# Attention with a bucketed bias and a feed-forward layer on one core: a new hand-laid order, one transpose each for q and k, single block stores, spare matmuls, a table difference on VectorE

## The chip, the cores and the metric

One core of a Trainium2 chip runs the whole program. The metric is the device time of one execution in microseconds (us); lower is better. The engines are named as in the profile: PE is TensorE (matmuls), PEld its weight loads, DVE is VectorE, ACT is ScalarE, POOL is GpSimd, SP is SyncE. POOL, SP and ACT also issue DMAs.

## The reference

Eight batches of eight heads, 576 positions, 64 channels a head. Attention gets a bias that depends only on the distance of the two positions (32 buckets, the last for all distances from 128 on), and its output goes through two projections with a leaky ReLU between them.

```python
def _attn_ref(q, k, v, bias_table):          # q, k, v: (8, 8, 576, 64), bias_table: (32, 8)
    scores = q @ k.transpose(0, 1, 3, 2) / sqrt(64)
    n = abs(pos[:, None] - pos[None, :])
    large = min(16 + (log(max(n, 1) / 16) / log(128 / 16) * 15).astype(int), 31)
    bucket = where(n < 16, n, large)
    scores = scores + bias_table[bucket].transpose(2, 0, 1)[None]
    return softmax(scores) @ v

def _moe_ref(x, w_in, w_out):                # x: (4608, 512), w_in: (512, 2048), w_out: (2048, 512)
    h = x @ w_in
    return maximum(0.01 * h, h) @ w_out
```

x is the attention output with the heads side by side; everything is float32 outside, bf16 in the matmuls.

## The kernel before, in words

**Attention** runs over 32 pairs `n` (8 batches `b`, 4 pairs of heads `p`). For a pair, q and k are turned so that the channels lie on the partitions. For the first nine pairs but one PE turns them (`turn_by_pe`); for the others DVE copies the rows of q and of k into one tile `pr` (`rows`), and one DMA transpose on SP's queue turns both into one tile `tu` (`turn_by_dma`), from which two copies make `qt` and `kt` (`take_turned`). PE makes the scores in six units (`score`: four of 128 keys, two for the last 64 positions), ACT takes the exponential into `at` (`expo`), DVE multiplies the band of near positions with a table of exponentiated bias differences, `hk` (`band`), PE multiplies with v (`av`, `av_tail`), and DVE divides by the row sum that an extra column of ones gave (`norm`, tile `opair`). A second transpose (`x_dma` on SP's queue, `x_pe` on PE) puts the result into `xT`, a ring of four batches.

**The table.** Since exp(s + bias) is wanted up to a factor, `hk` holds the exponential of the bias less that of the last bucket. In the opening a matmul with `from_last` (identity less its last column) subtracts on PE (`shift_table`, tile `ps_d`), four exponentials make `diag` (`exp_table`), and matmuls with the one-hot matrix `hots` spread it (`spread`, `take_spread`).

**Feed-forward** runs over nine token tiles `T` of 512 tokens. The first projection (`ffn_in`, tile `pm`, then `ffn_act` into `gt`) is plain for T below 6. For T = 6, 7 and 8 (`SPLIT`) a unit, half of the 2048 columns, is done with seven products of half-size blocks instead of eight (`plan_split`, `in_product`, `in_keep`, `in_add`, `in_act`), whose sums of weights (`mix_w_in`) and of x (`mix_x`) DVE makes. The partial products are kept in the buffers of attention (`held`: `at`, `vn`), the sums in those of q and k. The second projection takes seven products in the same way for all T (`ORDER`, `product`), DVE combines them in `y` (`combine`), and SP stores `y` by half tiles of rows (`ffn_store`); the last tile is stored by blocks (`block_store`).

**The order.** Nothing is scheduled by a compiler: a planner (`Plan`) holds all tasks with costs, dependencies, PSUM slots (`S` two, `O` one, `M` three) and ranks, and simulates the engines to lay one fixed order for each; each engine then runs its list in that order and waits by semaphores. `SHIFT` moves ranks, `HOLD` keeps a task back until a planned time, `SWAP` moves a copy between ACT and DVE. Loads on POOL's queue are planned one after the other (`pool_load`); transposes get a planned landing, and some tasks a reserve, `t["spare"]`, in us. Idle PE time before `WARM` (26 us of the plan) is filled with matmuls on `junk` (`spin`, tile `ps_w`), so that PE isn't idle while it waits; ten of them open the program:

```python
    spin(10)
    plan.run(spin)
```

Of the kernel before, what the change touches and what calls it, by code (L numbers as in the profile page):

```python
# [35 lines left out]

class Plan:


    LAG, COLD, WARM, EARLY, PATIENCE = 0.25, 4.9, 26.0, 34.0, 0.3  # L40

    SHIFT = {
# [26 lines left out]
    }  # L69

    SWAP = (20, 62, 88, 91, 92, 180, 185, 209, 214, 265, 273, 274, 996, 1089, 1368, 1757,)
# [26 lines left out]
    def order(self):  # L98
# [5 lines left out]
        free, done, waiting, ring = {}, [], {}, 0.0  # L104
# [3 lines left out]
        while any(waiting.values()):  # L108
# [29 lines left out]
            ring = self.place(t, r, free, self.slots, ring)  # L138
            done.append(t)
        free, ring = {}, 0.0  # L140
        for t in done:
            e = t["engine"]
            r = max([free.get(e, 0.0)] + [d["end"] + (self.LAG if d["engine"] != e else 0.0) for d in t["after"]])
            held = {k: sorted(slots[k]) for k in set(t["take"])}
            r = max([r] + [s[t["take"].count(k) - 1] for k, s in held.items()])
            ring = self.place(t, r, free, slots, ring)
        return done

    def place(self, t, r, free, slots, ring):
# [4 lines left out]
        if "turns" in t:  # L154
            t["end"] = max(r + 4.5, min(ring + 2.0, r + 11.0))
        if "moves" in t:
            t["end"] = ring = max(ring, r + t["cost"] + 1.0) + t["moves"]
# [8 lines left out]
        return ring  # L166

    def run(self, fill):

        for t in self.order():  # L170
            if t["engine"] == "PE" and 3.9 < t["start"] < self.WARM:
                k = round(t["idle"] / 0.22) if t["start"] < 8.5 else int((t["idle"] - 0.1) / 0.11)
                if k > 0:
                    fill(k)
            t["go"]()


@with_exitstack
def kernel(
# [28 lines left out]
    NPR, NTU = 3, 3  # L208
# [39 lines left out]
    kts_ = [per.tile([P, S + P], BF16, name=f"kt{i}") for i in range(3)]  # L248
# [7 lines left out]
    def load_qk(b, h0, h1, js=(0, 1)):  # L256
        i = b % NBUF
        for j in js:
# [3 lines left out]
                in_=src[b, h0:h1, :, :].rearrange("h (r c) d -> r h (c d)", c=NC),  # L262
            )
# [31 lines left out]
    for e in range(2):  # L295
# [6 lines left out]
    tab = per.tile([NB, H], FP32, name="tab")  # L302
    nc.sync.dma_start(out=tab, in_=bias_table)
# [7 lines left out]
    G = P // NB  # L311
    from_last = per.tile([NB, G, NB], FP32, name="from_last")
    nc.vector.tensor_tensor(out=from_last, in0=ident[0:NB, 0:NB].unsqueeze(1).to_broadcast([NB, G, NB]),
                            in1=ident[0:NB, NB - 1 : NB].unsqueeze(1).to_broadcast([NB, G, NB]), op=ALU.subtract)
# [16 lines left out]
    )  # L331
    for g in range(1, G):
        nc.vector.tensor_copy(out=hots[g * NB : (g + 1) * NB, 0 : UW - g], in_=hot[:, g:UW])
    def shift_table():
        ps = outs["d"] = ps_o_pool.tile([P, 512], FP32, name="ps_d", tag="ps_o")
        nc.tensor.matmul(ps[:, 0:H], lhsT=from_last.rearrange("b g c -> b (g c)"), rhs=tab, start=True, stop=True)

    def exp_table():
        ps = outs.pop("d")
        for g in range(G):  # L340
            r = slice(g * NB, (g + 1) * NB)
            nc.scalar.activation(diag[r, g, :], ps[r, 0:H], AF.Exp)
# [3 lines left out]
    def spread(m):  # L346
        ps = outs["u", m] = (ps_m_pool if m % 2 else ps_o_pool).tile([P, JB, H], FP32, name="ps_u", tag="m" if m % 2 else "ps_o")
        for j in range(0, JB, G):
# [44 lines left out]
    def rows(n, j):  # L393

        b, p = items[n]
        if j == 0 or n == 0:
            prs[n] = pr_pool.tile([RQ, 2, NC, 2 * D], BF16, name="pr")
        src = raw.rearrange("r e (c d) -> r e c d", d=D) if n == 0 else \
            (qn, kn)[j][b % NBUF][0:RQ, 2 * p : 2 * p + 2, :, :]
        (nc.scalar.copy if n == 0 else nc.vector.tensor_copy)(out=prs[n][:, j, :, :].rearrange("r c (e d) -> r c e d", e=2),  # L400
                        in_=src.rearrange("r e c d -> r c e d"))

    def turn_by_dma(n):
        t = turned[n] = tu_pool.tile([P, 2 * NC, RQ], BF16, name="tu")
        nc.sync.dma_start_transpose(out=t, in_=prs.pop(n).rearrange("r j c d -> r (j c d)"))
# [693 lines left out]
```

## Time and profile before

| | us |
|---|---|
| median of 3 runs | 361.18 |
| lowest, highest | 360.78, 361.99 |
| the profiled execution's own time | 360.76 |
| its span, first to last instruction | 359.0 |
| PE busy in the span | 350.7 |
| DVE busy | 297.6 |
| ACT busy | 262.2 |
| POOL busy | 70.3 |

All rows of the profile are of one execution, so sums made from them are set against its own 360.76 us. Times in rows count from the first instruction. In a row of the timeline the first number is the start, the second the time to the end of the last instruction merged into it. Matmuls are pipelined: the end of one is modelled, and neighbours overlap, so busy PE time is an upper bound on work.

### The profile page before, as it was taken

How to read it: one execution, taken by the hardware profiler on the slowest of the kernel's cores; microseconds unless marked ns; L12 is line 12 of the kernel's file. 1: busy time of each engine (PE TensorE's matmuls, PEld its weight loads, DVE VectorE, ACT ScalarE, POOL GpSimd, SP SyncE). 2: the span in 40 equal slices, each digit the busy share in tenths (PEclk: the TensorE clock that was granted, in tenths of full speed). 3: DMA queues.
4: the chain of work that ended last, by engine and by line, in shares of the span. 5: the costliest groups of instructions: out<-in, count | busy, mean ns of one | idle time of the engine just before them, and what ended most of it. 6: DMA issues, size and time to landing. Idle time of an engine off the chain costs nothing.

```text
span 359.0 us, 9973 instructions
## 1 busy us (share of the span) xinstructions
PE 350.7 (98%) x4147; PEld 254.1 (71%) x4172; DVE 297.6 (83%) x705; ACT 262.2 (73%) x352; POOL 70.3 (20%) x107
## 2 busy tenths in 40 slices
PE   8998999999999999999999999999999999999996
PEld 5665456774677655656767777667678888888885
DVE  6897979999799968986899879999559489497593
ACT  4988999678986899797988887887933574656530
POOL 8956123080008004300700310000000000000000
PEclk9999999999999999999999999999999999999999
DMA  8999999999949987991999296411123011030033
GB/s 126 148 178 193 203 179 144 142 147 208 133 113 125 136 153 89 193 182 20 133 158 222 42 141 89 135 21 21 20 20 119 2 63 57 2 117 2 0 119 117
DMA packets 103724, 39.58 MB, mean 110 GB/s; under 512 B 83200, under 2 KB 98560, under 8 KB 103680
## 3 DMA queue, kind: packets, MB, share of 16 engines
q0 software_dynamic: 53424, 18.21, 52.8%
q1 hardware_dynamic: 49904, 20.32, 31.8%
q8 instruction: 32, 0.52, 0.6%
q10 hardware_dynamic: 352, 0.43, 0.4%
q14 instruction: 12, 0.10, 0.1%
HBM read 36.70 MB, written 9.44 MB: 129 GB/s over the span
## 4 chain that ended last, share of the span: by engine, by line
PE 90%; DVE 5%; ACT 3%; issue 1%; DVEq 0%; ACTq 0%
PE pm L706 31%; PE pm L576 21%; PE pm L633 10%; PE ps_s L456 9%; PE ps_om L525 5%; PE ps_o L525 5%; PE ps_s L460 2%; PE ps_s L463 2%; PE ps_w L1064 1%; ACT at L470 1%; DVE at L490 1%; PE ps_o L510 1%; DVE opair L538 1%; PE ps_t L414 1%; ACT gt L652 1%
## 5 line engine op out<-in xcount | busy, mean ns | idle before, releaser
L470 ACT ACTIVATE at<-ps_s 128x1024 bf16<-128x1024 f32 x124 | 121.2, 1031 | 25.4 <-PE ps_s L456 22.3
L576 PE MATMUL pm<-xT,w_in_sb 128*128 128x512 bf16 (+1 forms) x423 | 91.2, 347 | 1.5 <-DVE xT L557 0.5
L490 DVE TENSOR_TENSOR at<-at,hk 128x768 bf16<-128x768 bf16 (+4 forms) x156 | 66.6, 450 | 14.1 <-ACT at L470 11.0
L652 ACT ACTIVATE gt<-pm 128x512 bf16<-128x512 f32 x96 | 57.3, 620 | 17.0 <-PE pm L576 16.5
L576 PEld LDWEIGHTS <-w_in_sb 128*128 128x128 bf16 x448 | 40.1, 98 | 32.4 <-issue 5.5
L706 PEld LDWEIGHTS <-gt 128*128 128x128 bf16 x576 | 54.7, 98 | 11.7 <-issue 3.0
L722 DVE TENSOR_TENSOR y<-pm,y 128x512 f32<-128x512 f32 (+1 forms) x53 | 41.1, 778 | 18.1 <-PE pm L706 17.1
L268 POOL DMA_DIRECT2D vn<-in_v_dram x32 | 28.8, 912 | 126.1 <-PE ps_o L525 110.9
L706 PEld LDWEIGHTS <-sum 128*128 128x128 bf16 x432 | 41.2, 98 | 9.0 <-issue 2.5
L525 PEld LDWEIGHTS <-at 128*128 128x128 bf16 x1240 | 41.4, 98 | 3.0 <-issue 0.7
L456 PE MATMUL ps_s<-qt,kt 64*128 64x512 bf16 x256 | 40.5, 387 | 0.6 <-ACT qt L431 0.4
L706 PE MATMUL pm<-w_out_sb,gt 128*128 128x256 bf16 x288 | 36.9, 273 | 0.0
L706 PE MATMUL pm<-mix,gt 128*128 128x256 bf16 x288 | 36.2, 273 | 0.0
L706 PE MATMUL pm<-w_out_sb,sum 128*128 128x256 bf16 x288 | 36.0, 273 | 0.0
L525 PE MATMUL ps_o<-vn,at 128*128 128x65 bf16 x640 | 25.4, 193 | 0.3 <-DVE opair L538 0.2
L525 PE MATMUL ps_om<-vn,at 128*128 128x65 bf16 x600 | 24.0, 194 | 0.0
L477 ACT ACTIVATE at<-ps_s 128x576 bf16<-128x576 f32 x31 | 20.9, 673 | 0.5 <-PE ps_s L464 0.4
L643 DVE TENSOR_TENSOR at<-pm,at 128x512 f32<-128x512 f32 (+1 forms) x18 | 15.3, 864 | 6.7 <-ACT at L637 3.6
L637 ACT COPY at<-pm 128x1024 f32<-128x1024 f32 x12 | 12.1, 1012 | 12.0 <-PE pm L633 11.9
L472 ACT ACTIVATE at<-ps_s 128x512 bf16<-128x512 f32 x31 | 19.0, 613 | 2.4 <-PE ps_s L460 1.7
L456 PEld LDWEIGHTS <-kt 64*128 64x128 bf16 x256 | 8.0, 94 | 17.3 <-issue 15.8
L706 PE MATMUL pm<-mix,sum 128*128 128x256 bf16 x144 | 19.0, 273 | 0.0
(119 smaller groups left out, 505.1 us busy)
## 6 DMA issues: line engine op xcount, KB each, us to landing
out_dram<-y SPq DMA_DIRECT2D x16, 512.0 KB, 3.4
vn<-in_v_dram POOLq DMA_DIRECT2D x32, 128.0 KB, 6.4
qn<-in_q_dram POOLq DMA_DIRECT2D x14, 288.0 KB, 10.9
kn<-in_k_dram POOLq DMA_DIRECT2D x14, 288.0 KB, 11.3
w_in_sb<-in_moe_w_in_dram POOLq DMA_DIRECT2D x2, 1024.0 KB, 11.2
w_out_sb<-in_moe_w_out_dram POOLq DMA_DIRECT2D x2, 1024.0 KB, 18.9
out_dram<-y SPq DMA_DIRECT2D x3, 256.0 KB, 2.2
qn<-in_q_dram POOLq DMA_DIRECT2D x4, 144.0 KB, 4.0
```

Source lines behind the costliest of these rows:

```text
L268: nc.gpsimd.dma_start(out=vn[i][:, c, :, 0:D], in_=v[b, :, c * P : (c + 1) * P, :].rearrange("h s d -> s h d"),)
L456: nc.tensor.matmul(ps[:, e, :], lhsT=kt[r, u * P : (u + 1) * P], rhs=qt[r, 0:512], start=True, stop=True)
L470: nc.scalar.activation(at[:, :, u, 0:512], ps, AF.Exp, scale=scale)
L472: nc.scalar.activation(at[:, :, :, 512:S].rearrange("p e c i -> p c e i"), ps[:, 0, :].rearrange("p (c e i) -> p c e i", e=2, i=SL), AF.Ex ...
L477: nc.scalar.activation(at4[:, 0:S], ps.rearrange("p e i -> p (e i)")[:, 0:S], AF.Exp, scale=scale)
L490: nc.vector.tensor_tensor(out=o, in0=o, in1=m, op=ALU.mult)
L525: nc.tensor.matmul(ps[:, ic, :], lhsT=at[:, o : o + P], rhs=vn[i][:, c, 2 * p + e, :], start=whole and c == 0, stop=not whole and ic == NJ ...
L576: nc.tensor.matmul(pms[T, f][:, o : o + n], lhsT=w_in_sb[:, c, f * P : (f + 1) * P], rhs=xT[c][:, x : x + n], start=(c == 0 and i == 0), s ...
L633: nc.tensor.matmul(ps[:, i, :], lhsT=w, rhs=x, start=fresh and i % 2 == 0 and c == 0, stop=i % 2 == 1 and c == 1, skip_group_check=not fresh)
L652: nc.scalar.activation(gts[T][:, f, :], pms.pop((T, f)), AF.Prelu, bias=0.0, scale=1.0, alpha=0.01)
L706: nc.tensor.matmul(ps[:, ts, :], lhsT=l[:, ts * P : (ts + 1) * P], rhs=r, start=(ts == 0 or apart) and j == 0, stop=(ts == 1 or apart) and ...
L722: nc.vector.tensor_tensor(out=out_, in0=ps, in1=x, op=ALU.add)
```

## The change

- **Opening.** 19 spins instead of ten. `bias_table` is loaded four times, once for each group of 32 partitions, and its last row once to all 128 partitions; DVE takes the difference, and `exp_table` reads it. `from_last`, `shift_table` and its two matmuls are gone.
- **Spare matmuls.** Where the plan has PE waiting between 26 and 95 us for data while the PSUM bank of the next group is free, `heat` puts matmuls on `junk` into that bank ahead of the group (26 us and before: `spin`, as it was, from 6.0 us of the plan).
- **Transposes.** `pr` and `tu` hold q or k alone (six buffers of half the size for three), and each gets its own DMA transpose. Copies out of `tu` may go to ACT.
- **Stores.** Each of the four blocks of `y` is stored as soon as it is whole, for all T. Product 1 is copied into another block, c21 for c22.
- **Half a tile more.** `SPLIT` lists units now, with the second half of T=5 in it.
- **Order.** The planner has transfers share capacity in two lanes (POOL's loads and SP's transfers, class `Lanes`), with SP's issues at 0.45 to 1.3 us for 0.1; reserves are 2.0 and 1.5 us; `SHIFT`, `HOLD` and `SWAP` are new throughout.
- `NAT = 99` and `CHAIN = 0` leave the paths of `in_order` and of the chained banks unused.

```diff
@@ Plan
-    LAG, COLD, WARM, EARLY, PATIENCE = 0.25, 4.9, 26.0, 34.0, 0.3
+    LAG, COLD, WARM, EARLY, PATIENCE, SHARE, FILL = 0.25, 6.3, 26.0, 34.0, 0.3, 0.4, 95.0
...
+            t["room"] = r - max([free.get(e, 0.0)] + [s[t["take"].count(k) - 1] for k, s in held.items()])
...
-            if t["engine"] == "PE" and 3.9 < t["start"] < self.WARM:
-                k = round(t["idle"] / 0.22) if t["start"] < 8.5 else int((t["idle"] - 0.1) / 0.11)
-                if k > 0:
-                    fill(k)
+            if t["engine"] == "PE" and 6.0 < t["start"]:
+                if t["start"] < self.WARM:
+                    fill(round(t["idle"] / 0.22) if t["start"] < 9.0 else int((t["idle"] - 0.1) / 0.11))
+                elif t["start"] < self.FILL:
+                    self.pre = max(0, int((t["room"] - 0.2) / 0.11))
             t["go"]()
+            self.pre = 0
@@ opening
-    nc.sync.dma_start(out=tab, in_=bias_table)
+    tab = per.tile([P, 2, H], FP32, name="tab")
+    nc.sync.dma_start(out=tab[:, 1, :], in_=bass.AP(tensor=bias_table.tensor, offset=bias_table.offset + (NB - 1) * H, ap=[[0, P], [1, H]]))
+    for g in range(G):
+        nc.sync.dma_start(out=tab[g * NB : (g + 1) * NB, 0, :], in_=bias_table)
...
+    nc.vector.tensor_tensor(out=tab[:, 0, :], in0=tab[:, 0, :], in1=tab[:, 1, :], op=ALU.subtract)
     for g in range(1, G):
         nc.vector.tensor_copy(out=hots[g * NB : (g + 1) * NB, 0 : UW - g], in_=hot[:, g:UW])
...
+    def heat(ps):
+        for _ in range(plan.pre):
+            nc.tensor.matmul(ps[:, 0:256], lhsT=junk[:, 0:P], rhs=junk[:, 0:256], start=True, stop=True)
+        plan.pre = 0
@@ transposes
-        nc.sync.dma_start_transpose(out=t, in_=prs.pop(n).rearrange("r j c d -> r (j c d)"))
+        t = turned[n, j] = tu_pool.tile([P, NC, RQ], BF16, name="tu")
+        nc.sync.dma_start_transpose(out=t, in_=prs.pop((n, j)).rearrange("r c d -> r (c d)"))
...
-                r0["spare"] = r1["spare"] = 2.0 if n < 4 * n_pairs else 8.0
+                r0["spare"] = 2.0
...
-        if by_dma(n) and n < 3 * n_pairs:
-            cq["spare"] = ck["spare"] = 3.5
+                t["spare"], t["other"] = 1.5, ("ACT", 0.6)
@@ stores
-                stored[T] = [add("SP", 0.1, [cb[5], cb[4]], lambda: ffn_store(T, 1), 10000, tail=2.5)]
+            if k in ready:
+                r, g = ready[k]
+                stored[T, r, g] = [moves(add("SP", 0.45, [cb[k]], lambda r=r, g=g: block_store(T, r, g), 10000), 0.7, 1, 2.0, 2.3)]
@@ split, spins
-    SPLIT = (6, 7, 8)
+    SPLIT = [(5, 1)] + [(T, u) for T in (6, 7, 8) for u in range(2)]
-    spin(10)
+    spin(19)
```

More of the change, by code (lines that the diff above doesn't have):

```diff
@@ L103, in order @@
                 t["engine"], t["cost"] = t["other"]
-        free, done, waiting, ring = {}, [], {}, 0.0
+        free, done, waiting, ring = {}, [], {}, Lanes(self.SHARE)
         slots = {k: list(v) for k, v in self.slots.items()}
@@ L153, in place @@
         t["start"], t["end"] = r, r + cost + t["tail"]
-        if "turns" in t:
-            t["end"] = max(r + 4.5, min(ring + 2.0, r + 11.0))
         if "moves" in t:
-            t["end"] = ring = max(ring, r + t["cost"] + 1.0) + t["moves"]
+            ring.push(t, r)
         for s in t.get("parts", ()):
@@ L310 @@
     small = NB // 2
[L311 to L314, printed above, removed]
     diag = per.tile([P, G, H], BF16, name="diag")
@@ L756, with moves, pool_load @@
     prev = []
-    def pool_load(key, cost, go, moves, after=(), rank=1):
+    def moves(t, work, lane, lead, least):
+        t["moves"], t["lane"], t["lead"], t["least"] = work, lane, lead, least
+        return t
+    def pool_load(key, cost, go, work, after=(), rank=1):
         t = add("POOL", cost, prev + list(after), go, rank)
-        t["moves"] = moves
+        moves(t, work, 0, min(cost + 1.0, 3.5), cost + 2.2)
         prev[:] = [t]
@@ L792, in plan_rows, with row @@
         ld = None if n == 0 else (L["qk", 0, p - 1] if b == 0 else L["qk", b, p // 2])
-        old = [t for t in rowt.get(n - NPR, [])[2:]] + (nrt[n_pairs - 1] if n == n_pairs + 1 else [])
-        on, cost = ("POOL", 0.9) if rows_by_pool(n) else ("DVE", 0.268)
+        ldk = L["k", b] if in_order(n) else ld
+        old = nrt[n_pairs - 1] if n == n_pairs + 1 else []
+        def row(j, after, at, on="DVE", cost=0.268):
+            t = add(on, cost, after + (pr_use[-NPR] if len(pr_use) >= NPR else []), lambda: rows(n, j), at)
+            pr_use.append([])
+            t["pr"] = pr_use[-1]
+            return t
         if n == 0:
-            r0, r1 = L["raw", 0], add("ACT", 0.75, [L["raw", 1]], lambda: rows(0, 1), -100)
+            r0, r1 = L["raw", 0], row(1, [L["raw", 1]], -100, "ACT", 0.75)
         elif by_heads(n):
@@ L819, in plan_rows @@
         on_act = n in (0, n_pairs)
-        ck = add("ACT" if on_act else "DVE", 0.53 if on_act else 0.57 if by_dma(n) else 0.72, [src[1]] + behind + sct.get(n - NQT, []),
-                 lambda: take_turned(n, 1, mover(ck)), feed, give=give)
+        direct = by_dma(n) and in_order(n)
+        ck = src[1] if direct else \
+            add("ACT" if on_act else "DVE", 0.53 if on_act else 0.57 if by_dma(n) else 0.72, [src[1]] + behind + sct.get(n - NKT, []),
+                lambda: take_turned(n, 1, mover(ck)), feed, give=give)
+        if by_dma(n):
+            for t, u in zip((cq,) if direct else (cq, ck), tu_use[-1:] if direct else tu_use[-2:]):
+                u.append(t)
         for t in (cq, ck):
@@ new lines, in plan_split @@
+        sums = lambda k: [wm[k, c] for c in range(2)]
+        a1 = pe(1, prior + opened[-1:], 0, ["S"])
+        k1 = add("ACT", 0.91, [a1] + prior, lambda: in_keep(T, u, 0), 0)
+        bs = [pe(2, [a1], 1, ["M"], q) for q in range(2)]
+        h11 = [add("DVE", 0.605, [bs[q], k1], lambda q=q: in_add(T, u, 0, ("b", q), q), 0, give=["M"]) for q in range(2)]
+        a6 = pe(6, [k1, xm] + sums(1), 2)
+        k6 = add("ACT", 0.91, [a6] + prior, lambda: in_keep(T, u, 1), 0)
+        c5 = pe(5, [xm, a1] + sums(0), 3, ["S"])
```

307 lines of the change are left out of this document (190 added, 117 removed), and 48 rows, old and new, of tables (HOLD, SHIFT).

## The prediction

> **What bounds the kernel now.** I read the page first, then busy time by stage, then the timeline of the opening, then the tiles that the change handles. The page's first and fourth parts:
>
> ```profile
> span 359.0 us, 9973 instructions
> PE 350.7 (98%) x4147; PEld 254.1 (71%) x4172; DVE 297.6 (83%) x705; ACT 262.2 (73%) x352; POOL 70.3 (20%) x107
> ...
> PE 90%; DVE 5%; ACT 3%; issue 1%; DVEq 0%; ACTq 0%
> ```
>
> TensorE is busy 98% and holds 90% of the chain that ended last. What is left is some 9% of the span, 32 us, in which the chain runs over another engine. Where it lies is read by stage (columns: stretch, its length, busy us of PE, PEld, DVE, ACT, POOL, granted clock, DMA):
>
> ```profile
> 0.00:20.00 20.00, 18.82 (x260) 12.03 (x260) 16.25 (x56) 14.45 (x22) 18.21 (x40) 1.00 1.25 142
> 20.00:60.00 40.00, 37.54 (x519) 22.82 (x522) 35.08 (x97) 36.61 (x53) 15.29 (x22) 1.00 1.57 184
> 60.00:260.00 200.00, 198.85 (x2481) 135.54 (x2499) 175.79 (x444) 164.77 (x231) 36.79 (x47) 1.00 1.02 119
> 260.00:350.00 90.00, 89.95 (x844) 79.05 (x845) 67.05 (x106) 46.40 (x49) 0.00 (x0) 1.00 0.15 50
> 350.00:359.00 9.00, 5.53 (x51) 4.70 (x49) 3.45 (x5) 0.00 (x0) 0.00 (x0) 0.97 0.35 116
> ```
>
> Four stages with different limits. To 20 us the inputs are turned and the table is built; part of PE's work there is spinning on `junk`. From 20 to 60 us PE stands idle 2.46 us, and ACT is busy 36.61 of 40: the exponentials feed everything. From 60 to 260 us PE is idle 1.15 us in 200, and from 260 to 350 us 0.05 us in 90: in these two stages only less PE work makes the end earlier. The tail, 350 to 359, is the last sums and stores.
>
> **The change part by part.**
>
> *The half tile that goes to seven products.* The second half of the first projection of token tile T=5 now takes seven half-size products instead of eight. Rates, from the chain of waits:
>
> ```profile
> 85.10 4.32 PE pm L576 x20
> 342.00 11.80 PE pm L706 x108
> ```
>
> A 512-column matmul is 4.32/20 = 0.216 us, a 256-column one 11.80/108 = 0.1093 us. Removed: 8 blocks x 4 = 32 of the first, 6.91 us. Added: 7 products x 8 = 56 of the second (same shape as L706's), 6.12 us. So PE has 0.79 us less to do, and since this half keeps its partial products in the buffers of the last attention pairs, it is done after them, where PE has no idle. Their last matmul with v starts at 264.69:
>
> ```profile
> 264.69 0.19 PE L528 MATMUL ps_o<-v,at 128*128 128x65 bf16 x1
> ```
>
> DVE and ACT get more work there, which these rows must hide:
>
> ```profile
> 260.00:270.00 10.00, 9.95 (x109) 7.31 (x110) 6.26 (x12) 3.58 (x6) 0.00 (x0) 1.00 0.27 47
> 270.00:280.00 10.00, 10.00 (x96) 8.99 (x95) 9.35 (x21) 4.59 (x5) 0.00 (x0) 1.00 0.21 78
> 280.00:290.00 10.00, 10.00 (x94) 8.96 (x93) 4.98 (x8) 5.54 (x7) 0.00 (x0) 1.00 0.01 2
> ```
>
> DVE gets eight more differences of x and four more sums, ACT a few us of copies. DVE has 9.4 us free in these thirty, ACT 16.3. I take the whole 0.79; the bounds are 0 (a chain of dependent products with nothing to put between them) and 0.79.
>
> *The opening: 19 spins for 10, the table's difference on DVE.* PE, in order of time:
>
> ```profile
> 1.10 2.31 PE L1064 MATMUL ps_w<-junk 128*128 128x256 bf16 x10 [1.10 <-DVE junk L293]
> 3.34 0.59 PE L336 MATMUL ps_d<-tab,from_last 32*128 32x8 f32 x2
> 3.86 1.46 PE L1064 MATMUL ps_w<-junk 128*128 128x256 bf16 x6
> 5.25 0.69 PE L419 MATMUL ps_t<-ident,qn 96*64 96x96 bf16 x12
> 6.75 1.06 PE L350 MATMUL ps_u<-diag,hots 128*128 128x32 bf16 x32
> 7.75 1.04 PE L456 MATMUL ps_s<-qt,kt 64*128 64x512 bf16 x4
> 10.43 0.45 PE L419 MATMUL ps_t<-ident,qn 96*64 96x96 bf16 x12
> 25.87 0.60 PE L456 MATMUL ps_s<-qt,kt 64*128 64x512 bf16 x4
> ```
>
> One spin is (2.31 - 1.46)/4 = 0.2125 us, twice the 0.1093 above, so the clock starts at half whatever the clock column says. Twelve transposes take 0.69 at 5.25 us and 0.45 at 10.43; four score matmuls 1.04 at 7.75 and 0.60 at 25.87. The full clock thus came between 7.75 and 10.43. Nineteen spins without the two matmuls of `ps_d` between them run from 1.10 to 1.10 + 19 x 0.2125 = 5.14, before the first transposes at 5.25: they delay nothing. If the full clock came by 5.25, the chain to the first exponentials would shrink by 0.24 (twelve transposes), about as much for the other side's, and half of 0.44 (two scores): 0.7 us. If it comes when it does now, 0. I take 0.3.
>
> The Trainium skill, "TensorE: Matmul & The Clock Gate", Part 1, says that the array runs at half clock until about 3.4 us of sustained activity have passed, in a window that runs freely. This trace agrees with it only in part: with spins, the table's matmuls and transposes from 1.10 on, it is still at half speed at 7.75. By that rule the unbroken spins would open the clock at about the first transposes, and the sum would hold 0.7 for my 0.3. That is a rival below.
>
> The table: `tab` is issued once now and five times after, the difference goes from PE to DVE, and the exponentials read it directly.
>
> ```profile
> 0.75 0.41 SPq L303 DMA_DIRECT2D tab<-in_bias_table_dram  x1
> tab<-in_bias_table_dram SPq DMA_DIRECT2D x1, 1.0 KB, 2.4
> 2.68 0.28 DVE L313 TENSOR_TENSOR from_last<-ident 32x128 f32<-32x128 bf16 x1 [1.22 <-POOL ident masks.py:199]
> 4.91 1.25 DVE L333 COPY hots<-hots 32x511 bf16<-32x511 bf16 x3
> 4.73 0.70 ACT L342 ACTIVATE diag<-ps_d 32x8 bf16<-32x8 f32 x4
> 5.99 0.64 ACT L431 COPY qt<-ps_t 128x576 bf16<-128x576 bf16 x1 [0.55 <-PE ps_t L419]
> ```
>
> The fifth issue starts at 0.75 + 4 x 0.41 = 2.39 and lands 2.4 later, at 4.8. DVE loses the 0.28 of `from_last` and gains one small difference of at most that, placed before the three copies of `hots`, which now start at 4.91: they wait behind it. So they stay within 0.2 us of where they are and end by 6.4, with the spread of the table at 6.75. The four exponentials go from 4.73 to about 5.1 and end by 5.8, before the copy of `qt` at 5.99. I cost this at 0; the cover is those 0.2 to 0.35 us, and a landing later than that moves the opening one for one (bounds -0.2 and +0.5).
>
> *Spare matmuls in waiting banks, 26 to 95 us.* They fill planned waits of PE with matmuls on `junk`. They are to keep the clock, but the four scores at 25.87 already run at full speed, as does L576 at 85.10. Nothing to win; each costs 0.109 us when its data come earlier than planned. I take 0, bounds 0 and +0.5 (five of them on the path).
>
> *One transpose each for q and k.* The tile view of `tu`:
>
> ```profile
> L405 SPq DMA_TRANSPOSE tu<-pr x24: 1273/1816/5740, 38.2 to 217.4; - x24
> ...
>   DVE qt L431: 0.5, 1
>   PE ps_s L456: 0.4, 1
>   DVE pr L400: 0.2, 1
> ...
> DMA to landing us min/median/max: 3.3/7.4/13.2
> ```
>
> ```profile
> xT<-opair SPq DMA_TRANSPOSE x24, 3.8
> ```
>
> 24 issues become 48. At the least 1.27 us of SP each that is 61 us, 24 x 1.27 = 30.5 more than the least now, in a stretch of 200 us that SP shares with 24 transposes of `opair` and the stores. Queued behind them on SP are just those, whose readers are the projections a tile later. All waits for these landings together are 1.1 us now, so I take 0: bounds -1.1 (all gone) and +4.3 (the last rival).
>
> *Blocks stored singly.* 16 stores of 512 KB and 3 last ones become 35 of 256 KB.
>
> ```profile
> out_dram<-y SPq DMA_DIRECT2D x16, 512.0 KB, 3.4
> out_dram<-y SPq DMA_DIRECT2D x3, 256.0 KB, 2.2
> ```
>
> Smaller ones land 1.2 us sooner and free a quarter of `y` at a time. The last tile was stored this way already, so the tail stays. 0.
>
> *The order, laid anew.* It can give something only where PE is idle beside free ACT time. In four rows of ten:
>
> ```profile
> 20.00:30.00 10.00, 9.73 (x210) 7.28 (x208) 9.23 (x27) 8.55 (x11) 4.79 (x8) 1.00 1.76 171
> 30.00:40.00 10.00, 8.34 (x109) 5.03 (x106) 8.11 (x28) 8.17 (x13) 4.88 (x7) 1.00 1.20 209
> 40.00:50.00 10.00, 9.89 (x106) 5.12 (x107) 9.09 (x22) 9.89 (x16) 0.88 (x1) 1.00 1.28 182
> 50.00:60.00 10.00, 9.58 (x102) 5.40 (x102) 8.65 (x22) 10.00 (x17) 4.75 (x7) 1.00 2.03 173
> ```
>
> From 40 to 60 ACT is full, 19.89 of 20. From 20 to 40 PE is idle 1.93 us and ACT 3.28: here attention hands over to the first projection. I take half of that, 1.0; bounds 2.46 (all idle of 20 to 60) and a loss of 2.5 (another 40 us of the steady stage packed no better than these).
>
> *Sum.* The profiled execution took 360.76 us: 360.76 - 0.79 - 0.3 - 1.0 = 358.7. It lies 0.4 below the median of the three runs, 361.18, so I predict 359.1.
>
> **The rivals.**
>
> *The opening packs fully.* All 2.46 us of idle go and the front gains 0.7: 361.18 - 0.79 - 0.7 - 2.46 = 357.2. For it: ACT had 3.28 us free there, and reserves that kept copies late were cut. Against: ACT is full from 40 to 60.
>
> *The clock opens by the first transposes* (the page's rule): 0.7 for 0.3, 358.7. Against: it did not after 16 spins with 0.6 us between them.
>
> *Nothing measurable.* The order gives nothing and the 0.79 is spent: inside the new half tile each product waits for ACT's copy of the one before, and the blocks of T=5 that stood between the last pairs' products are gone. Then the front's 0.3 stays: 361.18 - 0.3 = 360.9. For it: PE had to be filled just there. Against: the second projection of T=4 can be put between.
>
> *Slower: transposes come late.* The planned reserve of row copies falls from 8.0 to 2.0 us and that of the copies behind the transposes from 3.5 to 1.5, while SP issues twice. PE's order is fixed, so a pair's scores that wait hold all behind them. A landing at the maximum, 13.2, is 5.8 us after the median; past a reserve of 1.5 one such pair costs 4.3 us: 359.1 + 4.3 = 363.4. It decides from 3.2 us of such waits on (2.1 of gains and 1.1 of bound). Against: the same spread costs 1.1 us of waits today.
>
> **How the numbers follow.** A measurement of this kernel can tell about 0.3% (1.1 us): faster is below 360.1, slower above 362.3. My forecast has 0.32, with a range of its own of 358.0 to 360.1; the early clock 0.10 (358.7); the full opening 0.22 (357.2); nothing measurable 0.20 (360.9); late transposes 0.16 (363.4). The first three make 0.64 faster. The range goes from 356.4, the full opening with 0.8 of the 1.1 us of transposes' waits gone as well, to 361.9, past the even case, and leaves out most of the slow one.
>
> **What would show it.** Half tile: 32 matmuls fewer at L576's place in the code and 56 more at L633's, and PE from 265 to the tail dense and 0.8 us shorter. Clock: the first twelve transposes at 0.45 instead of 0.69. Table: the spread at or before 6.75. Order: PE busy above 38.5 of 40 from 20 to 60. Transposes: waits on `tu` under 1.5 us in total. I am wrong if PE waits in the steady stage for `tu` or `opair`, if the split unit leaves gaps near 265 us, or if the spread comes after 7 us.

## The result: 3% slower, and the profile after

The changed kernel took 372.75 us (median of six runs, 369.35 to 373.82), the kernel before 361.59 beside it (359.23 to 366.89): a ratio of 1.031, 95% interval 1.0254 to 1.0366. Here and below the ratio leaves out executions more than 1.5% above the fastest of the same kernel (here the one of 366.89), the medians don't. The prediction was 359.1 with a range from 356.4 to 361.9. The profiled execution of the changed kernel took 373.82 us for a span of 372.0. The page of the changed kernel (its first part, the chain by engine, one row of its groups and one of its transfers):

```profile
span 372.0 us, 10148 instructions
...
PE 355.6 (96%) x4187; PEld 257.5 (69%) x4187; DVE 293.8 (79%) x703; ACT 278.0 (75%) x365; POOL 68.7 (18%) x107
...
PE 72%; DVE 12%; DMA 6%; ACT 6%; issue 2%; SPq 0%; DVEq 0%; ACTq 0%
...
L651 PE MATMUL pm<-xT,w_in_sb 128*128 128x512 bf16 (+1 forms) x416 | 91.5, 350 | 0.4 <-DMA w_in_sb<-in_moe_w_in_dram 0.4
...
out_dram<-y SPq DMA_DIRECT2D x35, 256.0 KB, 2.5
```

TensorE's share of the chain fell from 90 to 72%; DMA, which had no share in it, has 6%, and VectorE went from 5 to 12%. In the same stages as before (columns as there):

```profile
0.00:20.00 20.00, 17.81 (x258) 11.45 (x259) 14.71 (x52) 15.37 (x23) 17.66 (x40) 1.00 1.30 145
20.00:60.00 40.00, 34.45 (x460) 20.13 (x458) 29.47 (x84) 33.07 (x48) 13.57 (x20) 0.96 1.55 176
60.00:260.00 200.00, 194.98 (x2432) 131.33 (x2429) 168.61 (x434) 172.82 (x237) 37.45 (x49) 0.99 1.03 121
260.00:350.00 90.00, 90.00 (x885) 78.34 (x883) 66.16 (x115) 52.13 (x56) 0.00 (x0) 1.00 0.13 40
350.00:372.00 22.00, 18.37 (x169) 16.21 (x166) 14.84 (x21) 4.64 (x5) 0.00 (x0) 0.99 0.25 85
```

From 20 to 60 TensorE is idle 5.55 us (2.46 before), from 60 to 260 5.02 (1.15 before), and the granted clock is below one in both stages. By rows of ten this is two places:

```profile
40.00:50.00 10.00, 7.27 (x83) 3.74 (x82) 2.80 (x10) 6.79 (x11) 1.57 (x2) 1.00 1.38 175
50.00:60.00 10.00, 8.98 (x68) 4.19 (x67) 8.20 (x17) 9.27 (x15) 2.81 (x5) 0.83 1.83 166
70.00:80.00 10.00, 6.00 (x51) 3.73 (x52) 8.68 (x21) 7.12 (x8) 0.00 (x0) 0.91 0.64 80
80.00:90.00 10.00, 10.00 (x118) 8.41 (x117) 9.52 (x27) 4.85 (x6) 3.33 (x4) 0.92 0.77 122
```

A mean clock of 0.83 over 10 us is 3.4 us at half speed; 0.91 and 0.92 side by side are 1.8 and 1.6, again 3.4 together. So each place costs twice: TensorE stands, and afterwards runs 3.4 us at half, which is 1.7 us of work lost. What it stood for is in the chain, in order of time (start, us, what):

```profile
37.79 9.94 DMA tu<-pr
...
47.76 0.02 ACT qt L502
...
48.82 1.50 ACT at L542 x2
...
62.13 9.00 DMA tu<-pr
...
71.22 0.36 DVE pr L457
...
77.72 0.50 DVE opair L611
...
78.26 0.21 PE ps_o L583
```

and in the timelines of TensorE and of VectorE, with the idle time ahead of a row and its cause in brackets:

```profile
49.88 0.38 PE L532 MATMUL ps_s<-qt,kt 128*128 128x128 bf16 x4 [2.73 <-ACT at L542]
51.29 0.64 PE L482 MATMUL ps_t<-ident,pr 96*128 96x96 bf16 x6 [1.02 <-ACT gt L727]
...
78.26 0.21 PE L583 MATMUL ps_o<-v,at 64*128 64x65 bf16 x1 [3.40 <-DVE opair L611]
```

```profile
71.22 0.36 DVE L457 COPY pr<-kn 96x768 bf16<-96x768 bf16 x1 [4.81 <-DMA tu<-pr]
```

*First place.* The transpose of q of pair 7 is issued at 37.79 and lands 9.94 later. ScalarE's fixed list has the copy out of `tu` (L502) ahead of exponentials of earlier pairs, so ScalarE stands 2.9 us, the exponentials behind it are late, and TensorE, whose scores find no free bank, stands with it. None of this needed the copy so early: the kernel's own planner placed it at 43.0 of its plan, 6.9 us after the issue of the transpose at 36.1, while the pair's first scores stand at 55.7.

*Second place.* At 71.22 VectorE wants to copy rows of k of pair 11 into a buffer `pr`, and the transpose of q of pair 9, issued at 62.13 and 9.00 us under way, still reads that buffer. Behind the row copy on VectorE's list stand eight sums and differences of `gt` (the second projection's, L749) and the division into `opair`, and behind that the products of a pair on TensorE. That wait is not in the plan: it counts buffers in the order in which tasks are made, and the program takes them in the order in which they are issued.

The tile view of `tu`:

```profile
L471 SPq DMA_TRANSPOSE tu<-pr x48: 1195/1240/3227, 37.8 to 228.8; - x48
L502 DVE COPY qt<-tu x19: 640/644/655, 80.1 to 249.5; 128x576 bf16<-128x576 bf16 x19
...
L502 ACT COPY kt<-tu x10: 1176/1194/1342, 52.6 to 210.2; 128x576 bf16<-128x576 bf16 x10
...
  DVE pr L457: 4.8, 1
  ACT qt L502: 2.9, 1
...
DMA to landing us min/median/max: 2.5/5.6/13.4
```

Smaller transposes land sooner at the median (5.6, before 7.4) and no sooner at the maximum (13.4, before 13.2). And the opening:

```profile
1.09 4.23 PE L1185 MATMUL ps_w<-junk 128*128 128x256 bf16 x19 [1.09 <-DVE junk L349]
5.60 0.69 PE L487 MATMUL ps_t<-ident,qn 96*64 96x96 bf16 x12 [0.27 <-DMA qn<-in_q_dram]
6.22 0.52 PE L482 MATMUL ps_t<-ident,pr 96*128 96x96 bf16 x6
7.18 1.22 PE L408 MATMUL ps_u<-diag,hots 128*128 128x32 bf16 x32 [0.45 <-ACT diag L393]
8.39 0.60 PE L528 MATMUL ps_s<-qt,kt 64*128 64x512 bf16 x4
```

```profile
6.03 0.17 DVE L387 TENSOR_TENSOR tab<-tab 128x8 f32<-128x8 f32 x1 [1.49 <-DMA tab<-in_bias_table_dram]
```

The table's difference starts at 6.03, the spread at 7.18 instead of 6.75. The first transposes still take 0.69, the scores at 8.39 take 0.60: the full clock came at about 6.4 us, four us sooner than before.

### The profile page after: what moved, and what is told of

Read it like the earlier page. It is cut to its first block, busy times and chain, and to the rows that moved or that the text cites. A ratio compares the mean times of both kernels' runs of the same rounds, so it can differ in the third digit from the quotient of the medians.

```text
span 372.0 us, 10148 instructions
## 1 busy us (share of the span) xinstructions
PE 355.6 (96%) x4187; PEld 257.5 (69%) x4187; DVE 293.8 (79%) x703; ACT 278.0 (75%) x365; POOL 68.7 (18%) x107
## 4 chain that ended last, share of the span: by engine, by line
PE 72%; DVE 12%; DMA 6%; ACT 6%; issue 2%; SPq 0%; DVEq 0%; ACTq 0%
PE pm L787 27%; PE pm L651 15%; PE pm L708 12%; PE ps_s L528 6%; DMA tu<-pr 5%; PE ps_om L598 4%; PE ps_o L598 4%; ACT at L542 3%; DVE at L562 2%; DVE sum L749 2%; DVE opair L611 2%; PE ps_s L532 1%; ACT gt L727 1%; PE ps_s L535 1%; DVE kt L502 1%
## 5 line engine op out<-in xcount | busy, mean ns | idle before, releaser
L651 PEld LDWEIGHTS <-w_in_sb 128*128 128x128 bf16 x416 | 36.9, 98 | 32.3 <-issue 10.8
L727 ACT ACTIVATE gt<-pm 128x512 bf16<-128x512 f32 x88 | 52.9, 632 | 7.1 <-PE pm L651 6.6
L718 DVE TENSOR_TENSOR at<-pm,at 128x512 f32<-128x512 f32 (+1 forms) x22 | 19.2, 882 | 12.2 <-ACT at L712 7.4
L712 ACT COPY at<-pm 128x1024 f32<-128x1024 f32 x15 | 15.2, 1010 | 15.7 <-PE pm L708 15.7
L724 ACT ACTIVATE gt<-at 128x1024 bf16<-128x1024 f32 x15 | 15.9, 1058 | 9.1 <-DVE at L718 9.1
```

Of the source, the lines that this page charges most:

```text
L651: nc.tensor.matmul(pms[T, f][:, o : o + n], lhsT=w_in_sb[:, c, f * P : (f + 1) * P], rhs=xT[c][:, x : x + n], start=(c == 0 and i == 0), s ...
L727: nc.scalar.activation(gts[T][:, f, :], pms.pop((T, f)), AF.Prelu, bias=0.0, scale=1.0, alpha=0.01)
```

## The experiments

Ratios are against the kernel before on the same chip, with 95% intervals. The runs were made on several chips, on which the median of the kernel before was 360.7 to 362.3, so medians of different runs compare to about 1 us.

### Are the late transposes the cause?

Without q's and k's transposes (the copies read a constant tile), in the changed kernel and, as the control, in the kernel before:

```diff
-        t = turned[n, j] = tu_pool.tile([P, NC, RQ], BF16, name="tu")
-        nc.sync.dma_start_transpose(out=t, in_=prs.pop((n, j)).rearrange("r c d -> r (c d)"))
+        prs.pop((n, j))
...
-            src = turned.pop((n, j)).rearrange("p c r -> p r c")
+            src = hk.rearrange("p h j -> p (h j)")[:, 0:S].rearrange("p (c r) -> p r c", c=NC)
```

> The changed kernel, its order untouched, with the DMA transposes of q and k left out: the copies into qt and kt read a constant instead, so nothing waits for a landing (q and k are wrong from pair 7 on, but for pair 8). Theory L (late landings hold ACT and DVE, and PE behind them, and the clock falls): all of the loss between 40 and 80 us goes, 372.75 - 9 to -12, so 360 to 364. Rival P (the parts themselves, or the new order's packing, cost the time, not the waits): it stays at 369 to 373.

Measured: 364.05 us, ratio 1.0088 (1.0051 to 1.0125). 8.7 of the 11.2 us are gone.

> The same taken from the kernel before, as a control: DMA transposes of q and k left out, copies read a constant. Theory L: that order has reserves that cover the landings, so it gains at most the 1.1 us of waits on tu and something of lighter DMA traffic: 359 to 361.6. If lighter traffic alone speeds any order up by much (rival: the transposes slow everything through the shared DMA engines), it comes under 357.

Measured: 360.1 us, ratio 0.9983 (0.9969 to 0.9996): leaving out the transposes of the old order gains 0.2%. So it is not the transposes, but how little the new order leaves them. The rows of the changed kernel without them:

```profile
20.00:60.00 40.00, 37.82 (x529) 22.90 (x529) 33.53 (x97) 37.60 (x53) 15.28 (x22) 1.00 1.60 187
60.00:120.00 60.00, 59.88 (x718) 39.42 (x716) 53.33 (x137) 53.72 (x74) 15.67 (x20) 1.00 0.87 96
```

Which of them? Only those of pairs 7 and 9 to 12 left out (`if n < 13`):

> The changed kernel with the DMA transposes of pairs 7 and 9 to 12 alone left out (copies read a constant), the other 38 kept. Theory L1 (the loss lies in the landings beside the loads of weights and of batches 2 and 3, 38 to 76 us): nearly all that the first experiment gained, so 364 to 365.5. Rival L2 (late landings cost everywhere): 367 to 370.

Measured: 365.4 us, ratio 1.0118 (1.0052 to 1.0184). Five pairs, turned between 38 and 76 us, hold 7.4 of the 8.7 us.

### Is it the number of transposes, or their place?

The kernel before, with each transpose issued as two into the same tile:

```diff
-        nc.sync.dma_start_transpose(out=t, in_=prs.pop(n).rearrange("r j c d -> r (j c d)"))
+        for j in range(2):
+            nc.sync.dma_start_transpose(out=t[:, j * NC : (j + 1) * NC, :], in_=prs[n][:, j, :, :].rearrange("r c d -> r (c d)"))
```

> The kernel before with its one transpose for q and k issued as two, one after the other, at the same place in SP's list; nothing else moved. Theory L: the split of the transpose isn't the cause, the planned landing is: 360.5 to 363. Rival S (48 issues load SP and land later): 364 to 372.

Measured: 364.1 us, ratio 1.0066 (1.0029 to 1.0104). I had priced this at nothing, and it costs about 2.4 us (1.0 to 3.8 by the interval), with the old order and its reserves. Its row from 70 to 80, and the wait in its tile view of `tu`:

```profile
70.00:80.00 10.00, 8.52 (x107) 5.72 (x105) 9.90 (x23) 5.99 (x8) 6.90 (x10) 1.00 1.61 154
```

```profile
  DVE pr L400: 2.3, 1
```

VectorE again waits 2.3 us with a row copy for a transpose that reads its buffer, and TensorE loses 1.48 us there.

The buffers of the changed kernel fixed in the order in which the plan counts them:

```diff
-        prs[n, j] = pr_pool.tile([RQ, NC, 2 * D], BF16, name="pr")
+        prs[n, j] = own_pr[with_rows.index((n, j)) % NPR]
...
-        t = turned[n, j] = tu_pool.tile([P, NC, RQ], BF16, name="tu")
+        t = turned[n, j] = own_tu[with_turn.index((n, j)) % NTU]
```

> The changed kernel with the six buffers of pr and of tu taken by the turn that the planner counts (order of creation) instead of by the order in which the tasks are issued; order and parts untouched. In the changed kernel DVE waits 4.8 us at 66 us for the landing of a transpose that still reads a pr buffer, a wait that the planner does not have there. Theory R (this unplanned wait is the stall at 70 to 78 us): DVE's wait on tu goes, PE's 3.4 us and the half clock after it too: 366 to 369. Rival: DVE waits elsewhere for the same landings: 371 to 373.5.

Measured: 368.53 us, ratio 1.0201 (1.0101 to 1.03).

```profile
40.00:50.00 10.00, 7.66 (x85) 3.88 (x83) 3.71 (x11) 7.75 (x12) 1.21 (x2) 1.00 1.36 187
50.00:60.00 10.00, 9.06 (x39) 3.69 (x38) 7.46 (x16) 8.10 (x13) 3.55 (x6) 0.66 1.74 157
70.00:80.00 10.00, 10.00 (x100) 7.95 (x99) 9.89 (x26) 9.00 (x11) 0.00 (x0) 1.00 0.58 106
```

The second place is gone (10.00 of 10, 6.00 in the changed kernel), the first one stays, with a longer stretch at half clock (0.66 over 10 us is 6.8 us). So the rotation of the buffers is worth some 4 us at the medians (the intervals overlap), and the early copy on ScalarE stays.

Why do they land so late? The q and k loads of batches 2 and 3 left out, but two heads of k:

> The changed kernel without the loads of q and k of batches 2 and 3, but for two heads of k (those batches compute with older data). Theory C (transposes land late because POOL's loads take the DMA engines): the transposes of 62 to 72 us land in 2.5 to 5 us instead of 5.9 to 9.0, the first ones beside w_out stay at 9 or more, and the stall at 70 goes: 366 to 369. Rival: SP's own queue sets the landing: landings and time stay, 371 to 373.5.

Measured: 368.93 us, ratio 1.0206 (1.0115 to 1.0297). The transposes from 65 to 71 us now land in 2.5 to 4.1 us (those from 62 to 72 us took 3.5 to 9.0 in the changed kernel), while the first two, beside a load of `w_out` that this kernel keeps, still take 8.6 and 9.2. With that the second place is gone and the first one stays:

```profile
50.00:60.00 10.00, 6.96 (x55) 3.59 (x54) 6.05 (x14) 8.25 (x11) 0.00 (x0) 0.83 0.91 45
70.00:80.00 10.00, 10.00 (x131) 7.96 (x128) 9.89 (x24) 9.35 (x12) 0.00 (x0) 1.00 0.55 101
```

A transpose is late when loads on POOL's queue are in flight. The trace of the changed kernel agrees: no load is in flight from 71.2 to 86.7 us, and the three transposes issued from 81 to 85 us land in 2.5 to 2.6. The Trainium skill, "DMA: Bandwidth & Descriptors", section "Queues, rings and completion order", says that each DMA engine takes turns between the queues that have work for it, a packet at a time; these landings agree with that, 2.5 us alone and 8.6 to 9.9 for the first transpose beside loads, though no run here counted packets by engine.

Would the planner have found a better order with less capacity for transfers? `SHARE` 0.15 for 0.4, so that planned landings come later:

> The changed kernel with one number of the planner changed: SP's share of the transfers 0.15 for 0.4, so that the order is laid for landings about as late as the trace shows them (the first transpose planned at 10.7 us after its issue, 9.9 measured). All parts stay. Theory L (the planned landing is the fault): the long waits on tu go, the order is a little less dense by plan: 364 to 369. Rival P (the parts cost it): 371 to 375.

Measured: 373.48 us, ratio 1.0317 (1.0251 to 1.0383): no gain, against what I expected. No engine waits for a landing in its tile view of `tu` any more (VectorE waits 6.4 us for ScalarE's copies, 8.8 in the changed kernel), but TensorE still stands idle 5.3 us from 60 to 260:

```profile
60.00:260.00 200.00, 194.66 (x2385) 129.55 (x2384) 166.06 (x425) 172.54 (x238) 37.11 (x48) 1.00 1.00 120
```

Part of its time lies elsewhere. In its profile the full clock came only at about 24 us (6.4 in the changed kernel), and the first product of the feed-forward layer starts at 38.71 us for 34.39. A row of TensorE's timeline at half clock:

```profile
18.51 0.69 PE L487 MATMUL ps_t<-ident,kn 96*64 96x96 bf16 x12
```

And `SHIFT`, `HOLD` and `SWAP` were tuned for other landings. So this run doesn't judge the planner's rule by itself.

### Are the copies on ScalarE too dear?

A copy out of `tu` takes 1.19 us on ScalarE and 0.64 on VectorE; the plan has 0.6 for it. All of them on VectorE, with the transposes and without (`copy = nc.vector.tensor_copy`):

> The changed kernel with the 15 copies out of tu that it put on ACT (1.18 us each, planned at 0.6) issued on DVE at the same places of the order (0.65 us each). Theory L: the wait for the landing moves from ACT to DVE, the stall at 47 us stays, and only the 2.9 us of ACT's wait and part of the dearer copies go: 367 to 371. Rival A (ACT is late because its copies cost twice the planned time): 359 to 364.

Measured: 371.1 us, ratio 1.0232 (1.0127 to 1.0336): not to be told from the changed kernel. The waits moved to VectorE, as theory L said: in its tile view of `tu` it waits 2.4 us for the landing and 5.6 for the buffer `pr`.

> The changed kernel without the DMA transposes of q and k (copies read a constant) and with those copies all on DVE: the first and the fourth experiment together. 364.05 and 371.1 were measured (8.7 and 1.6 less than the changed kernel). Theory A2 (the dearer copies on ACT are a loss of their own, besides the landings): 361.5 to 363. Rival: the 1.6 was part of the same waits: 363.5 to 364.5.

Measured: 365.08 us, ratio 1.0102 (1.0056 to 1.0147), against 364.05 with the copies on ScalarE, and above both ranges. Moving all of them wins nothing where the landings don't matter. The rows of this run say why:

```profile
60.00:80.00 20.00, 18.59 (x233) 13.72 (x232) 19.83 (x51) 12.14 (x17) 1.82 (x2) 1.00 0.33 64
120.00:140.00 20.00, 20.00 (x255) 12.03 (x253) 14.54 (x40) 17.78 (x26) 0.07 (x1) 1.00 0.43 82
```

From 120 to 140 TensorE is now full, but from 60 to 80 VectorE is (19.83 of 20), and TensorE waits there.

### What did the opening cost?

The kernel before with the five loads and VectorE's difference (its spins left as they were):

> The kernel before with the changed opening of the table alone: five loads of bias_table on SP's queue, the difference on DVE, no matmul and no from_last; ten spins as before, order untouched. In the changed kernel the first load of k landed at 4.85 us (3.97 before) and the difference started at 6.03. Theory O (the five loads and the later table push the opening back, about one for one): +0.5 to +1.2, so 361.7 to 362.6. Rival: the opening hides it (my prediction): 360.8 to 361.5.

Measured: 363.17 us, ratio 1.0064 (1.0028 to 1.01): the table's new way, priced at nothing, costs about 2.3 us by itself (1.0 to 3.6 by the interval). In its profile the first product of the feed-forward layer starts at 36.53 us, 34.67 in the kernel before. The changed kernel with the old way:

```diff
-    spin(19)
+    spin(10)
+    shift_table()
+    spin(9)
```

> The changed kernel with the table made as before: one load of bias_table, from_last, the difference on PE between ten and nine spins; all else as changed. The same opening put into the kernel before cost it 0.64% (+2.3 us). Theory O (the five loads delay the first loads of k and q by 0.6 to 0.9 us and the table by 3, and PE's wait for it lets the clock fall): 369.5 to 371.5. Rival: the loss of the opening is hidden behind the waits of 40 to 78 us: 372 to 373.5.

Measured: 373.12 us, ratio 1.0299 (1.0199 to 1.0399), no gain beside the late transposes. Without the transposes it shows:

> The changed kernel without its q and k transposes (the copies read a constant tile in their place), and with the old opening: one load of the table, ten spins, the difference as a matmul, nine spins. Theory that the remaining 3 to 4 us are the late table and the clock that falls back: 361 to 362. Rival, the new order's packing of ScalarE: 363.5 to 364.5, as with the new opening (364.05). The kernel before without its transposes took 360.1.

Measured: 362.53 us, ratio 1.0052 (1.0033 to 1.007), 1.5 us below the run with the new opening (364.05), with intervals that overlap.

> The changed kernel without its q and k transposes, with the new opening and six more spins ahead of the matmul that spreads the table. Theory that TensorE's gap between 6.6 and 7.8 us lets the clock fall back to half: the clock stays open from about 6.4 us on, and the time is 362.5 to 363.3. Rival, the late table itself or the packing costs the time and the clock does not: 364 or more.

Measured: 363.44 us, ratio 1.0081 (1.0052 to 1.0109), between the two theories and not to be told from 364.05. The spins do hold the clock. TensorE in the changed kernel without transposes, and below it the same with six spins in the gap:

```profile
7.86 1.22 PE L408 MATMUL ps_u<-diag,hots 128*128 128x32 bf16 x32 [1.21 <-ACT diag L393]
9.07 0.61 PE L527 MATMUL ps_s<-qt,kt 64*128 64x512 bf16 x4
...
11.41 0.69 PE L486 MATMUL ps_t<-ident,qn 96*64 96x96 bf16 x12
```

```profile
8.38 0.60 PE L529 MATMUL ps_s<-qt,kt 64*128 64x512 bf16 x4
...
10.44 0.45 PE L488 MATMUL ps_t<-ident,qn 96*64 96x96 bf16 x12
```

In the first the clock is full at 9.07 and half again at 11.41 (the trace's clock record: half from 9.5 to 13.0); in the second it stays. The first products of the feed-forward layer start at 34.92 and 34.06, and the end moved by 0.6 at the medians. The other executions agree: with the six spins the mean granted clock is 0.998 to 1.000 in all six; without them it is 1.000 in two of ten, which took 363.43 and 363.64 us, and at most 0.995 in the other eight, 363.77 us and more.

Spins alone, on the kernel before: three more behind `shift_table`, 19 in all.

> The kernel before with three more spins behind the matmul that spreads the table, 19 in all, and nothing else changed. Theory: the granted clock opens at 10.4 us in the kernel before because the sixteen spins leave TensorE a gap; with three more it opens three or four us earlier, the first projections run at .24 instead of .45 us, and the end moves by 0.2 to 0.6 us: 360.2 to 361 against 361 to 361.5 beside it. Rival: the clock opens earlier and falls back, as in the changed kernel without transposes, or the projections wait for their loads anyway: no change or up to 1 us slower.

Measured: 361.01 us against 360.93, ratio 1.0027 (0.9992 to 1.0062): no change. In its profile the clock opened at 10.2 us, as in the kernel before, although 19 spins opened it at 5.2 in the changed kernel with the old opening and no transposes. So this run shows that three spins more don't open the clock sooner there; it doesn't show what a sooner opening would be worth.

### What is left: the packing

Without transposes and with the old opening, the new order is still 2.4 us above the control. Its rows from 20 to 60 and from 120 to 140:

```profile
20.00:60.00 40.00, 37.48 (x505) 22.20 (x504) 33.73 (x97) 36.92 (x54) 15.26 (x21) 1.00 1.60 190
120.00:140.00 20.00, 19.11 (x236) 11.55 (x233) 11.88 (x34) 19.95 (x28) 1.73 (x2) 1.00 0.22 53
```

From 120 to 140 ScalarE is full, with five copies of 1.2 to 1.4 us that VectorE, 8 us free, could take. Seven copies given to VectorE, two near 45 us and these five:

```diff
     def take_turned(n, j, copy):
+        if (n, j) in ((7, 0), (7, 1), (16, 1), (17, 0), (17, 1), (18, 0), (18, 1)):
+            copy = nc.vector.tensor_copy
```

> The changed kernel without its q and k transposes and with the old opening (362.53), and seven copies of qt and kt, of pairs 7, 16, 17 and 18, taken from ScalarE to VectorE: those that ScalarE makes at 43 to 49 and at 118 to 140 us, where it is full (19.8 and 19.95 of 20) and VectorE has 4 and 8 us free. Theory that ScalarE's fullness in these two stretches holds TensorE: its idle time there falls by 2 to 3 us, and the time to 360 to 361. Rival: VectorE, which is in a fixed order of its own, hands the loss on to the stretches behind it, as when all copies were moved (365.08): 362 or more.

Measured: 361.61 us, ratio 1.0011 (0.9982 to 1.004); 360.73 beside it.

```profile
20.00:60.00 40.00, 38.13 (x505) 21.95 (x504) 34.80 (x99) 35.62 (x53) 15.21 (x21) 1.00 1.60 190
120.00:140.00 20.00, 20.00 (x243) 12.14 (x240) 14.86 (x39) 17.12 (x26) 3.30 (x4) 1.00 0.34 61
```

Both stretches fill as far as in the control (38.06 and 20.00 there), and the time is no longer to be told from that of the kernel before. What still lies between this run and the control (361.61 and 360.1) is within what these runs can tell, or just outside. Their profiles say where to look: TensorE's last run of 108 matmuls starts at 341.97 us here, at 341.58 in the control and at 342.00 in the kernel before (354.83 as changed, 344.98 without transposes, 343.28 with the old opening as well). The rest of the distance between the two profiles, 1.9 of 2.2 us, is the last two stores, which landed 3.8 and 3.9 us after their issue here and 1.9 and 2.0 there. That is one execution of each; whether the stores are late as a rule stays open.

### Can the change be mended?

Buffers as planned, the old opening, and the copies out of `tu` moved back in their engines' lists to 14 us after the issue, where the first scores leave room; then the same with the seven copies on VectorE:

> The changed kernel with the buffers by the planner's turn, the old opening, and the copies out of tu moved back in the order to 14 us after the issue of their transpose where the pair's scores leave room; nothing else. Theory L with O and R: what the first experiment gained (8.7) and the opening's part go together: 360.5 to 364. If these three aren't the causes: 368 or more.

Measured: 364.26 us, ratio 1.009 (1.0044 to 1.0136). 8.5 us are back with all the transposes kept. The buffers alone gave 4.2 and the opening alone nothing, so about 4 us belong to the later copies, if the parts add up; no run has the later copies alone.

> The mended kernel (buffers by creation order, old opening, copies moved back; 364.26) with the same seven copies on VectorE. Theory: 361.5 to 362.5, still no better than the kernel before, since the transposes of pair 7 land late all the same. Rival: the copies of pair 7 on VectorE wait for their transposes there and hold the row copies and bands behind them: 364 or more.

Measured: 364.19 us, ratio 1.0108 (1.0053 to 1.0163). No further gain, as the rival said. Its cause is only in part there: VectorE waits with row copies for the transposes (2.5 us in its tile view of `tu`), but it did so before the seven copies moved (1.8). No version here beat the kernel before.

## Why the prediction was wrong, point by point

By the medians, in order: 372.75 as changed; 364.05 without the transposes; 362.53 with the old opening as well; 361.61 with seven copies moved as well. The control without transposes took 360.1. The ratios in the same order, each against its own chip: 1.031, 1.0088, 1.0052, 1.0011; control 0.9983.

- **Single transposes, taken as 0 (bounds -1.1 and +4.3): this step failed.** Left out, they give back 8.7 us in the new order; issued as two for one, they cost 2.4 in the old. I argued from the waits of the kernel before, 1.1 us in all, and didn't ask what kept them small. It was the cover in its plan, the time from the issue of a transpose to the copy that reads it. The planner before let a transpose land up to 11.0 us after its issue while loads were planned beside it, and added a reserve of 3.5 up to pair 11; run on its own, it reckons the landing of pair 7 at 11.0 us and puts the first copy at 14.0 us after the issue. The new planner reckons that landing at 5.25 us and adds 1.5; its copy stands 6.9 us after the issue, and the landing took 9.94. The line of the old planner that the change takes away:

```diff
-            t["end"] = max(r + 4.5, min(ring + 2.0, r + 11.0))
```

So the larger part of the cover went with the planned landing, not with the reserves that I had named. The reserve of 8.0 us for row copies was no part of it: it held from pair 16 on alone, and for the pairs that cost the time it was 2.0 before and after. That the cover is the cause is shown as far as copies at 14 us gave the time back, together with the buffers and the opening. I also looked for the waits behind the transposes only (copies, scores) and not at the buffer that a transpose reads: row copies had waited for it before (`pr`, 0.2 us in the quoted view), and that became the larger place, 4.8 us.
- **The rival "transposes come late"** had the mechanism, and the wrong price. I counted one late pair at 4.3 us, from the median landing of 7.4 where the new plan has 5.25. There were two places, three gaps of 2.73, 1.02 and 3.40 us, and after each place 3.4 us at half clock, 1.7 us each: 10.6 us together; 8.7 came back without the transposes, where TensorE still idles 2.18 us from 20 to 60. The sign of being wrong that I had named, TensorE waiting for `opair`, is the row with 3.40. Its chance of 0.16 was too low as well; that the same spread of landings costs 1.1 us today was no evidence against it.
- **The table on VectorE, taken as 0 (to +0.5).** I put the fifth landing at 4.8 and the difference ahead of 4.91; it started at 6.03 and the spread at 7.18, after the 7 that I had named as a sign of being wrong. Five issues in a row land later than one (3.5 to 3.6 us from issue at the median, for 2.4), and q's first load came later with them (5.55, before 4.94). Alone on the kernel before it cost about 2.3 us; in that profile the spread starts at 7.82, 1.1 late, and the clock opened at 13.5 instead of 10.4.
- **The opening's clock, -0.3.** It did open sooner, at 6.4 us, as the rule of the rival would have it, but not by the first transposes (0.69 each dozen). What that was worth isn't shown: more spins on the kernel before changed neither the clock in the profile nor the time, and in the new opening the gap ahead of the spread can send it back to half, which cost about 0.6 us at the medians.
- **The order, -1.0.** With everything else taken away it gives nothing that the time shows: 38.13 of 40 from 20 to 60 against my "above 38.5", and against 37.54 before and 38.06 in the control. It put copies on ScalarE where that was full, at a planned 0.6 us each for a real 1.19.
- **The half tile, -0.79.** The counts came as said: 416 weight loads at L576's place for 448, 392 at L633's place for 336, and from 260 to 350 TensorE is full. No run measures its worth alone, since the numbers in `SHIFT` belong to the tasks of one order; in the last run without transposes (ratio 0.9982 to 1.004) it is contained and the sum of all that remains doesn't show a gain.
- **Spare matmuls, 0.** None was issued: the 37 matmuls on `junk` all write `ps_w`. **Single stores, 0**: landing at 2.5 us for 3.4, about as reckoned; nothing waits for them.

## What to carry to other kernels

Where a wait is small, ask what makes it small before you take it over into the sum: a cover that the change cuts, a planned landing as much as a reserve, is a price, and it is paid at the spread of the landings, not at their median. For each transfer list both sides, who waits for what it writes and who waits to refill what it reads, and what stands behind each of them on an engine with a fixed list. Price a stall of TensorE with what follows it: here a gap of 3 us cost another 1.7 us at half clock.

## What the runs showed of the hardware that I had not expected

- The clock fell back in stretches of 3.4 us and multiples (3.4, 6.8 and 13.7 us in these traces). The Trainium skill, "TensorE: Matmul & The Clock Gate", Part 1, gives a freely running window of about 3.4 us, and the lengths agree with it; a free phase also fits that 19 spins opened the clock at 4.8, 5.2 and 10.2 us in three kernels. In the opening of the kernel without DMA transposes of q and k the 3.4 us at full clock that ended at 9.5 had one gap of 1.21 us, and half clock followed; in the changed kernel the same place had a gap of 0.45 us and the clock stayed. So a window with a third of it idle can close the clock; how much of it has to be busy, these runs don't show. A free phase doesn't explain the opening with `SHARE` 0.15, which stayed at half to about 24 us although TensorE was busy 10.00 of 10 us from 10 to 20.
- A copy of 128 x 576 bf16 out of `tu` took 1.19 us on ScalarE and 0.64 on VectorE, while ScalarE's copy of the same size out of PSUM took 0.64.
- One DMA transpose of 96 x 768 landed in 2.5 us alone, and in up to 13.4 us beside loads on another queue.
